# An FFT-convolution block on one core: transposing the filter ssm_k as 32-bit words instead of as bf16 elements

## The chip, the cores and the metric

One core of one Trainium2 chip. The core has five engines that run side by side and wait for one another by semaphores: TensorE (PE, with its weight loads shown apart as PEld), VectorE (DVE), ScalarE (ACT), GpSimd (POOL) and SyncE (SP), which issues most DMAs. SBUF is the working memory, 128 partitions wide; PSUM is where TensorE writes. The metric is the device time of one execution in microseconds (us), less is better. A time is the median of several executions.

## The reference

Shapes: S = 2048 time steps, D = 512 channels, all inputs bf16. In short:

```
kv = causal_conv4(k, shift_k) * v                  # 4 taps in time, per channel
y  = irfft(rfft(kv, 4096) * rfft(ssm_k, 4096))[:S] # long convolution in time, per channel
y  = y + kv * ssm_D
h  = q + layernorm(q) * y
out = h + relu(layernorm(h) @ w1) @ w2             # w1: 512 x 1376, w2: 1376 x 512
```

ssm_k is the long filter, 512 channels by 2048 steps. What this document is about is the start of the kernel, where ssm_k is read and brought into the layout that the Fourier transform needs.

## The kernel before

The program is written out in order by hand; each engine executes its own instructions in the order in which the code issues them, and waits where data or a place is missing. The stages that matter here:

- **Start (L95 to L252).** SP loads ssm_k into the tile `sk` (128 partitions x 4 channel groups x 2048 steps) in one DMA of 2 MB (L96). It then issues eight transposing DMAs, alternately for k (`kT`) and v (`vT`), a chunk of 512 steps each, and two small loads for ssm_D. While ssm_k loads, PE multiplies zeros (22 products, L110). POOL makes an identity (`ident`, L156 and L157), the tap matrices `wdiag` (L235), the first transform's tables `f1hi`, `f1lo`, `f2hi`, `f2lo`, and the negated sine table `c2n` (L247). DVE works out the angles for the sine tables (`cs_turns` L194, `_turns` L42, `cc_turns` L217, with `wrap` L186), and ACT evaluates sines (`table` L189, `_sin` L139).
- **Transposing ssm_k (L274 to L326).** `to_rows` is called for q = 0 to 7. Each call transposes eight 128x128 bf16 blocks on PE: block i holds the elements with step number 8q + i modulo 64, so the columns read from `sk` lie 64 elements apart. The eight results fill one PSUM bank, and one copy takes them into `kfl`, on DVE for even q and on ACT for odd q. For q = 3 and 4 the PSUM place is one of the two banks (`pk0`, `pk1`) that the taps use afterwards; the others take three places in turn, so q = 5, 6 and 7 wait for the copies of q = 0, 1 and 2.
- **Second half of the angles (L327).** `cc_turns(16)`, two instructions on DVE (L219, L187), stands behind these copies in DVE's order; one sine instruction (L328) stands behind them on ACT.
- **Taps and first transform stage (L340 to L358).** Eight rounds. In each, `taps` makes the 4-tap convolution on PE, in two PSUM banks, and DVE multiplies the result by v (L347), writing kv over `sk`. Then `stage1` transforms a part of `kfl` on PE, and ACT and DVE copy the result to `a1k`. A round's taps need the two banks that the round before used, so they wait for its L347.
- **Transposing kv (L380 to L392).** kv was written in pairs of neighbouring steps, so that 128 pairs lie side by side. A pair of bf16 elements is transposed as one 32-bit word (`kv32`, with a 32-bit identity `ident32` made at L338), four blocks of words per PSUM bank. The results go to `xfl`: on DVE as int32 with an OR by zero (L386), for q = 0, 2, 3, 5, 7, and on ACT as bf16 in two copies (L392), for q = 1, 4, 6.
- **The rest**: second transform stage of the filter (L398), first and second stages of kv, the products with the filter's transform, the inverse transform, and the two matrix products of the MLP with its layer norms, to the output DMAs.

The lines that the steps of the prediction speak of most are these:

```python
            nc.tensor.transpose(out=pst[:, i, :], in_=src[:, :, :, 8 * q + i], identity=ident[:])   # L278
        copy(eng, fl[:, :, :, 8 * q:8 * q + 8], pst[:].rearrange("p i (d g) -> p g d i", d=2))     # L279
...
        to_rows(skv, q, kfl, "DADADADA"[q])                                                        # L326
    cc_turns(16)                                                                                   # L327
```

Of the kernel before, what the change touches and what calls it, by code (L numbers as in the profile page):

```python
# [9 lines left out]
ALU = mybir.AluOpType  # L10
BF16 = mybir.dt.bfloat16
F32 = mybir.dt.float32
F32R = mybir.dt.float32r
I32 = mybir.dt.int32
PSUM = bass.MemoryType.PSUM
P = 128
# [40 lines left out]
def kernel(  # L57
# [13 lines left out]
    nc = tc.nc  # L71
    _, S, D = A_q.shape
# [15 lines left out]
    early = pl.push("early")  # L88
# [6 lines left out]
    sk = early.tile([P, DC, S], BF16, name="sk")  # L95
# [23 lines left out]
    for dp in range(2):  # L119
        src = bass.AP(tensor=A_ssm_D.tensor, offset=A_ssm_D.offset + 64 * dp, ap=[[0, 64], [P, DC], [1, 64]])  # L120
# [29 lines left out]
    for s in range(0, P, 64):  # L150
# [4 lines left out]
    ident = consts.tile([P, P], BF16, name="ident")  # L155
    nc.gpsimd.memset(ident[:], 0.0)  # L156
    nc.gpsimd.affine_select(out=ident[:], in_=ident[:], compare_op=ALU.not_equal, fill=1.0,  # L157
                            base=0, pattern=[[-1, P]], channel_multiplier=1)

    n1c = early.tile([P, 1], F32, name="n1c")  # L160
    n2c = early.tile([P, 1], F32, name="n2c")
# [55 lines left out]
    def cc_turns(a):  # L217
        part = tcs[:, a:a + 16, :]
        nc.vector.tensor_single_scalar(out=part, in_=tsn[:, a:a + 16, :], scalar=2048.0, op=ALU.add)  # L219
        wrap(part, 8192)  # L220
# [33 lines left out]
    def copy(eng, o, i):  # L254
        if eng == "A":
            nc.scalar.copy(out=o, in_=i)  # L256
        else:
            nc.vector.tensor_copy(out=o, in_=i)  # L258
# [4 lines left out]
    def place(shape, dtype, name):  # L263
        i = ring.pop(0)
        ring.append(i)
        return places[i].tile(shape, dtype, tag=f"ps{i}", name=name)
# [4 lines left out]
    def tap_bank(i, shape, dtype, name):  # L271
        return psum_t.tile(shape, dtype, tag=f"pk{i}", name=name)

    def to_rows(src, q, fl, eng):  # L274
        shape = [P, 8, P]
        pst = tap_bank(q % 5 - 3, shape, BF16, "pst") if q % 5 > 2 else place(shape, BF16, "pst")
        for i in range(8):
            nc.tensor.transpose(out=pst[:, i, :], in_=src[:, :, :, 8 * q + i], identity=ident[:])  # L278
        copy(eng, fl[:, :, :, 8 * q:8 * q + 8], pst[:].rearrange("p i (d g) -> p g d i", d=2))  # L279

    def stage1(fl, a_out, gb, engs, pairs=False):

# [38 lines left out]


    kfl = early.tile([P, 64, 2, 64], BF16, name="kfl")
    skv = sk[:].rearrange("p c (a b) -> p c a b", b=64)
    for q in range(8):
        to_rows(skv, q, kfl, "DADADADA"[q])  # L326
    cc_turns(16)  # L327
    _sin(dsc[:], t3[:], 64)  # L328
    dre = consts.tile([P, 2, 2, 64], F32R, name="dre")
# [4 lines left out]


    kvp2 = sk[:].rearrange("p c t -> p (c t)").rearrange("p (m c a e) -> p m c a e", m=32, c=DC, e=2)
    ident32 = early.tile([P, P], F32, name="ident32")
    nc.gpsimd.tensor_copy(out=ident32[:], in_=ident[:])  # L338

    def taps(c, h):  # L340
        pss = [tap_bank(i, [P, 512], F32, "pkv") for i in range(2)]
        for i in range(2):
            for j in range(KS):
                nc.tensor.matmul(out=pss[i][:], lhsT=wdiag[:, 2 * h + i, j, :],  # L344
                                 rhs=kT[c][:, 2 * h + i, 16 - j:CH + 16 - j], start=(j == 0), stop=(j == KS - 1))
        for i in range(2):
            nc.vector.tensor_tensor(out=kvp2[:, :, 2 * h + i, 8 * c:8 * c + 8, :].rearrange("p m a e -> p a m e"),  # L347
                                    in0=pss[i][:].rearrange("p (a m e) -> p a m e", a=8, e=2),
                                    in1=vT[c][:, 2 * h + i, :].rearrange("p (a m e) -> p a m e", a=8, e=2),
                                    op=ALU.mult)  # L350
# [24 lines left out]
    pl.pop("kvp")  # L375
    xfp = pl.push("xfp", side="right")
    xfl = xfp.tile([P, 64, 2, 64], BF16, name="xfl")
    kv32 = sk[:].rearrange("p c t -> p (c t)").bitcast(F32).rearrange("p (m x) -> p m x", m=32)
    xfl32 = xfl[:].rearrange("p g d n -> p (g d n)").bitcast(I32).rearrange("p (g d m) -> p g d m", g=64, d=2)
    for q in range(8):  # L380
        pst = place([P, 4, P], F32, "pst2")
        for i in range(4):
            nc.tensor.transpose(out=pst[:, i, :], in_=kv32[:, 4 * q + i, :], identity=ident32[:])  # L383
        ms = slice(4 * q, 4 * q + 4)
        if "DADDADAD"[q] == "D":
            nc.vector.tensor_single_scalar(out=xfl32[:, :, :, ms],  # L386
                                           in_=pst[:].bitcast(I32).rearrange("p m (d g) -> p g d m", d=2),
                                           scalar=0, op=ALU.bitwise_or)
        else:
            src = pst[:].rearrange("p m x -> p (m x)").bitcast(BF16).rearrange("p (m d g e) -> p d g m e", m=4, d=2, e=2)  # L390
            for d in range(2):
                nc.scalar.copy(out=xfl[:, :, d, 8 * q:8 * q + 8].rearrange("p g (m e) -> p g m e", e=2), in_=src[:, d])  # L392
    pl.pop("early")
    pl.pop("vp")
    slotB = pl.push("slotB")
# [437 lines left out]
```

## Time and profile before

| what | value |
|---|---|
| time, median of 3 runs | 208.6 us (208.33 to 209.07) |
| the profiled execution | 209.07 us, of which the span from the first to the last instruction is 206.9 us |
| granted TensorE clock | 0.998 of full speed |
| busy in the span | PE 195.4 us (94%), PEld 139.8 (68%), DVE 147.7 (71%), ACT 129.7 (63%), POOL 84.8 (41%) |
| ssm_k's transpositions on PE | start at 8.76 us, last 5.91 us |
| first taps after them | start at 14.51 us |
| second taps | start at 18.18 us |
| kv's transpositions on PE | start at 36.58 us |

How to read it: times are counted from the first instruction of the profiled execution. An engine that is busy for 94% of the span need not do useful work at its peak, since matmuls are pipelined and a waiting one can count as busy. The chain of waits names, going back from the last instruction, what each step waited for, so it tells which engine sets the end at each moment. A group line gives the line of code, the engine, the operation, the tiles out<-in, their shapes, how many there are, then the busy time and the mean duration of one in ns, and last the idle time of the engine ahead of them with what ended it.

### The profile page before, as it was taken

The page shows a single profiled execution, that of the slowest core. Times are in us where ns is not written, and L with a number is a line of the kernel's source. Part 1 is how long each engine was busy: PE and PEld are TensorE (multiplying, and loading weights), DVE is VectorE, ACT ScalarE, POOL GpSimd, SP SyncE. Part 2 cuts the span into 40 slices and gives each one's busy share as a digit, 9 for nine tenths or more (in the row PEclk, how much of TensorE's full clock was granted, in tenths as well). Part 3 has the DMA queues.
Part 4 walks back from the last instruction along what each step waited for, and adds up shares of the span by engine and source line. Part 5 has one row for each costly group of instructions (what it writes and reads, how often), then busy time and mean ns, then how long its engine had stood idle before and what let it go on. Part 6 is the DMA issues. An engine that isn't in the chain of part 4 may idle for free.

```text
span 206.9 us, 4925 instructions
## 1 busy us (share of the span) xinstructions
PE 195.4 (94%) x2017; PEld 139.8 (68%) x2017; DVE 147.7 (71%) x237; ACT 129.7 (63%) x196; POOL 84.8 (41%) x121
## 2 busy tenths in 40 slices
PE   7797999999996999999999999999999999999992
PEld 2494545899876799887999877645565556544451
DVE  7998777977686999988996599698297208561131
ACT  2676899845696688886896975753580494026300
POOL 4699991000001999997769655230202001102000
PEclk9999999999999999999999999999999999999999
DMA  5999960000000004835992557783753502040011
GB/s 179 339 220 188 197 126 5 3 3 0 3 3 2 5 0 122 203 154 148 197 287 49 108 101 56 165 156 97 138 100 77 119 13 54 27 103 22 0 54 51
DMA packets 48490, 20.03 MB, mean 97 GB/s; under 512 B 43380, under 2 KB 46932, under 8 KB 48468
## 3 DMA queue, kind: packets, MB, share of 16 engines
q1 hardware_dynamic: 47940, 19.71, 43.6%
q8 instruction: 16, 0.26, 0.5%
q10 hardware_dynamic: 528, 0.00, 0.1%
q14 instruction: 6, 0.05, 0.1%
HBM read 7.08 MB, written 2.10 MB: 44 GB/s over the span
## 4 chain that ended last, share of the span: by engine, by line
PE 82%; DVE 11%; ACT 3%; issue 1%; POOL 0%; POOLq 0%; ACTq 0%
PE ps1m L705 19%; PE ps2m L735 19%; PE psy L453 7%; PE psi L600 7%; PE pkv L344 6%; PE ps L299 4%; PE ps2k L317 4%; PE ps2k L319 4%; PE u L317 3%; PE u L319 3%; PE pz L678 3%; DVE kfl L258 2%; PE pst L383 2%; ACT a1x L256 1%; DVE w_ts L196 1%
## 5 line engine op out<-in xcount | busy, mean ns | idle before, releaser
L720 ACT ACTIVATE h1T<-ps1m 128x512 bf16<-128x512 f32 (+1 forms) x44 | 25.7, 597 | 35.8 <-PE ps1m L705 35.7
L705 PE MATMUL ps1m<-xT,w 128*128 128x512 bf16 (+2 forms) x192 | 43.7, 365 | 0.4 <-DVE xT L651 0.4
L735 PE MATMUL ps2m<-w,h1T 128*128 128x512 bf16 (+3 forms) x187 | 40.8, 368 | 0.0
L678 PE MATMUL pz<-bd,ax 128*128 128x128 f32 x96 | 35.7, 410 | 0.0
L443 POOL TENSOR_TENSOR t<-usb,kf 128x320 fp32r<-128x320 f32 x32 | 28.2, 937 | 2.3 <-ACT usb L439 1.9
L443 DVE TENSOR_TENSOR t<-u,kf 128x704 fp32r<-128x704 f32 x32 | 26.7, 887 | 3.4 <-ACT usb L439 3.4
L739 DVE SCALAR_TENSOR_TENSOR o<-ps2m,rstd,xh 128x512 bf16<-128x512 f32 (+1 forms) x17 | 12.0, 717 | 21.6 <-PE ps2m L735 10.1
L735 PEld LDWEIGHTS <-h1T 128*128 128x128 bf16 (+1 forms) x187 | 16.3, 98 | 16.0
L544 POOL TENSOR_SCALAR rstd<-mv 128x4 f32<-128x4 f32 x8 | 2.5, 317 | 56.5 <-DVE mv L542 56.5
L705 PEld LDWEIGHTS <-w 128*128 128x128 bf16 (+1 forms) x192 | 15.9, 100 | 12.1 <-DVE xT L651 0.5
L678 PEld LDWEIGHTS pz<-bd,ax 128*128 128x128 f32 x96 | 18.6, 193 | 7.6
L649 DVE TENSOR_TENSOR qT<-pz,qT 128x1024 bf16<-128x1024 f32 x8 | 9.8, 1219 | 15.1 <-PE pz L678 7.3
L538 DVE BATCH_NORM_STATS2 st<-xh 128x6 f32<-128x512 bf16 x32 | 19.8, 677 | 0.0
L256 ACT CAST kf<-psy 128x512 fp32r<-128x512 f32 x30 | 17.5, 644 | 1.9 <-PE psy L453 0.3
L528 ACT ACTIVATE bd<-ecw,nbias 32x512 fp32r<-32x512 int32 x24 | 17.3, 719 | 0.6
L344 PE MATMUL pkv<-kT,wdiag 128*128 128x512 bf16 x64 | 15.2, 380 | 1.2 <-DVE sk L347 1.2
L453 PE MATMUL psy<-t,ipos 128*128 128x512 f32 x48 | 16.0, 393 | 0.0
L256 ACT CAST a1k<-ps 128x1024 fp32r<-128x1024 f32 x12 | 12.8, 1112 | 3.1 <-PE ps L299 3.1
L256 ACT CAST ax<-psi 128x1024 fp32r<-128x1024 f32 x13 | 12.4, 1017 | 3.7 <-PE psi L600 3.7
L600 PE MATMUL psi<-dre,kf 128*128 128x256 f32 x60 | 14.6, 286 | 0.0
L600 PE MATMUL psi<-dim,kf 128*128 128x256 f32 x60 | 14.3, 280 | 0.0
L347 DVE TENSOR_TENSOR sk<-pkv,vT 128x512 bf16<-128x512 f32 x16 | 10.8, 689 | 4.3 <-PE pkv L344 4.3
(136 smaller groups left out, 419.4 us busy)
## 6 DMA issues: line engine op xcount, KB each, us to landing
sk<-in_A_ssm_k_dram SPq DMA_DIRECT2D x1, 2048.0 KB
xh<-in_A_q_dram SPq DMA_DIRECT2D x16, 128.0 KB
out_dram<-o SPq DMA_DIRECT2D x15, 128.0 KB
w<-in_B_w_dram SPq DMA_DIRECT2D x1, 1376.0 KB
w<-in_B_w_dram SPq DMA_DIRECT2D x1, 1280.0 KB
xh<-xT SPq DMA_TRANSPOSE x8
out_dram<-o SPq DMA_DIRECT2D x2, 64.0 KB
w<-in_B_w_dram SPq DMA_DIRECT2D x1, 96.0 KB
```

Of the source, the lines that this page charges most:

```text
L256: nc.scalar.copy(out=o, in_=i)
L317: nc.tensor.matmul(out=ps[:, kk, :], lhsT=at_k1(w_re, k1), rhs=a_in[:, k1, :], start=True, stop=False, skip_group_check=True)
L344: nc.tensor.matmul(out=pss[i][:], lhsT=wdiag[:, 2 * h + i, j, :], rhs=kT[c][:, 2 * h + i, 16 - j:CH + 16 - j], start=(j == 0), stop=(j == ...
L443: eng.tensor_tensor(out=t[:, :, j, :], in0=in0.unsqueeze(1).to_broadcast([P, 2, n, 2]), in1=kfr[:, :, j, ks], op=ALU.mult)
L453: nc.tensor.matmul(out=psy[:], lhsT=m_[:], rhs=t_.rearrange("p j k -> p (j k)"), start=first, stop=not first)
L528: nc.scalar.activation(out=bd[h][rows, :, :, rg, :], in_=ecw[q % 2][rows, :, 256 * h:256 * h + 256].rearrange("p b (j n) -> p b j n", n=32 ...
L538: nc.vector.bn_stats(out=st[:, i, :], in_=src[:, i, :])
L600: nc.tensor.matmul(out=banks[i // 2][:, i % 2, :], lhsT=kf[:, c, 4 * m:4 * m + 4, :].rearrange("p r k -> p (r k)"), rhs=d[:].rearrange("p ...
L678: nc.tensor.matmul(out=pz[:, il, :, a, :], lhsT=ax[:, 64 * rho + n2, :, :].rearrange("p d g -> p (d g)"), rhs=bd[h][:, rho, 4 * il + a, :, ...
L705: nc.tensor.matmul(out=ps1[fc][:fsz, 128 * ii.start:128 * ii.stop].rearrange("p (i t) -> p i t", t=P), lhsT=w1[:, c, fc * P:fc * P + fsz], ...
L720: nc.scalar.activation(out=h1T[:fsz, fc, :], in_=ps1[fc][:fsz, :], func=ACT.Relu)
L735: nc.tensor.matmul(out=ps2[:, 0:w], lhsT=h1T[:ksz, fc, i * P:(i + 1) * P], rhs=w2[:ksz, fc, ds], start=(fc == 0), stop=(fc == NFC - 1))
```

## The change

ssm_k is transposed in the way in which kv already was: two neighbouring steps (2m and 2m + 1) are one 32-bit word. `to_rows` makes four transpositions of 128x128 words for each q, with the identity `ident32`, and moves the words on DVE (int32, OR with zero) or ACT (bf16, two copies). The words of one block are read from `sk` at a distance of 32 words, since ssm_k lies as it was loaded. `to_rows` now serves both transpositions, with the same split over DVE and ACT ("DADDADAD"), so for ssm_k five moves are on DVE and three pairs on ACT, in place of four copies on each. The conversion that makes `ident32` moves up to the place where `ident` is made. Nothing else changes; the transposition of kv issues the same instructions.

```diff
     nc.gpsimd.affine_select(out=ident[:], in_=ident[:], compare_op=ALU.not_equal, fill=1.0,
                             base=0, pattern=[[-1, P]], channel_multiplier=1)
+    ident32 = early.tile([P, P], F32, name="ident32")
+    nc.gpsimd.tensor_copy(out=ident32[:], in_=ident[:])
...
-    def to_rows(src, q, fl, eng):
-        shape = [P, 8, P]
-        pst = tap_bank(q % 5 - 3, shape, BF16, "pst") if q % 5 > 2 else place(shape, BF16, "pst")
-        for i in range(8):
-            nc.tensor.transpose(out=pst[:, i, :], in_=src[:, :, :, 8 * q + i], identity=ident[:])
-        copy(eng, fl[:, :, :, 8 * q:8 * q + 8], pst[:].rearrange("p i (d g) -> p g d i", d=2))
+    def to_rows(word, q, fl, eng):
+        shape = [P, 4, P]
+        pst = tap_bank(q % 5 - 3, shape, F32, "pst") if word is sk_word and q % 5 > 2 else place(shape, F32, "pst")
+        for i in range(4):
+            nc.tensor.transpose(out=pst[:, i, :], in_=word(4 * q + i), identity=ident32[:])
+        if eng == "D":
+            fl32 = fl[:].rearrange("p g d n -> p (g d n)").bitcast(I32).rearrange("p (g d m) -> p g d m", g=64, d=2)
+            nc.vector.tensor_single_scalar(out=fl32[:, :, :, 4 * q:4 * q + 4],
+                                           in_=pst[:].bitcast(I32).rearrange("p m (d g) -> p g d m", d=2),
+                                           scalar=0, op=ALU.bitwise_or)
+        else:
+            src = pst[:].rearrange("p m x -> p (m x)").bitcast(BF16).rearrange("p (m d g e) -> p d g m e", m=4, d=2, e=2)
+            for d in range(2):
+                nc.scalar.copy(out=fl[:, :, d, 8 * q:8 * q + 8].rearrange("p g (m e) -> p g m e", e=2), in_=src[:, d])
...
-    skv = sk[:].rearrange("p c (a b) -> p c a b", b=64)
+    sk32 = sk[:].rearrange("p c t -> p (c t)").bitcast(F32).rearrange("p (x m) -> p x m", m=32)
+    kv32 = sk[:].rearrange("p c t -> p (c t)").bitcast(F32).rearrange("p (m x) -> p m x", m=32)
+
+    def sk_word(m):
+        return sk32[:, :, m]
+
     for q in range(8):
-        to_rows(skv, q, kfl, "DADADADA"[q])
+        to_rows(sk_word, q, kfl, "DADDADAD"[q])
...
-    ident32 = early.tile([P, P], F32, name="ident32")
-    nc.gpsimd.tensor_copy(out=ident32[:], in_=ident[:])
...
     for q in range(8):
-        pst = place([P, 4, P], F32, "pst2")
...
+        to_rows(lambda m: kv32[:, m, :], q, xfl, "DADDADAD"[q])
```

More of the change, by code (lines that the diff above doesn't have):

```diff
@@ L377 @@
     xfl = xfp.tile([P, 64, 2, 64], BF16, name="xfl")
-    kv32 = sk[:].rearrange("p c t -> p (c t)").bitcast(F32).rearrange("p (m x) -> p m x", m=32)
-    xfl32 = xfl[:].rearrange("p g d n -> p (g d n)").bitcast(I32).rearrange("p (g d m) -> p g d m", g=64, d=2)
     for q in range(8):
-        pst = place([P, 4, P], F32, "pst2")
[L382 to L392, printed above, removed]
+        to_rows(lambda m: kv32[:, m, :], q, xfl, "DADDADAD"[q])
     pl.pop("early")
```

## The prediction

> **What bounds the kernel now.** I read the share of each engine first (PE 94%, DVE 71%, ACT 63%, POOL 41%), then the chain of waits over the first 37 us, because every line of the change that executes differently lies there. The chain, in order of time (start, length, what):
>
> ```profile
> 10.38 0.69 DVE w_tc L187
> 11.07 4.52 DVE kfl L258 x4
> 15.59 1.22 DVE w_tc L219
> 16.90 0.55 issue
> 17.45 0.69 DVE sk L347
> 18.18 1.89 PE pkv L344 x8
> ```
>
> The reader is to see that until 18.18 us the end is set by DVE: table arithmetic to 11.07, its four copies of transposed ssm_k, more table arithmetic (L219, then L187 from 16.84 to 17.53), and the first product L347. That product frees the PSUM bank that TensorE's second group of taps needs, so PE starts again at 18.18. From there on the chain is PE, nearly without a gap, and a shift of 18.18 passes to the end. The groups of instructions of this stage, and of the later stage that already transposes words, give the prices (busy us, mean ns | idle before):
>
> ```profile
> L278 PEld LDWEIGHTS <-sk 128*128 128x128 bf16 x64 | 5.8, 201 | 1.6 <-DMA sk<-in_A_ssm_k_dram 1.6
> L344 PEld LDWEIGHTS <-wdiag 128*128 128x128 bf16 x64 | 5.8, 98 | 7.2 <-issue 1.1
> ...
> L258 DVE COPY kfl<-pst 128x1024 bf16<-128x1024 bf16 x4 | 4.6, 1212 | 0.0
> L256 ACT COPY kfl<-pst 128x1024 bf16<-128x1024 bf16 x4 | 4.1, 1018 | 2.9 <-PE pst L278 2.9
> ...
> L383 PEld LDWEIGHTS pst<-ident,sk 128*128 128x128 f32 x32 | 3.4, 141 | 0.6 <-issue 0.3
> L386 DVE TENSOR_SCALAR xfl<-pst 128x512 int32<-128x512 int32 x5 | 3.4, 687 | 0.3
> ...
> L392 ACT COPY xfl<-pst 128x512 bf16<-128x512 bf16 x6 | 3.1, 596 | 0.5 <-DVE a1k L258 0.3 <-PE pst L383 0.2
> ```
>
> And two stretches of the timeline of PE (start, length, what, how many):
>
> ```profile
> 8.76 5.91 PE L278 MATMUL pst<-ident,sk 128*128 128x128 bf16 x64 [1.06 <-DMA sk<-in_A_ssm_k_dram]
> ```
> ```profile
> 36.58 1.06 PE L383 MATMUL pst<-ident,sk 128*128 128x128 f32 x8 [0.26 <-DVE sk L347]
> ```
>
> Each bf16 transposition takes (5.91-0.25)/63 = 0.09 us, each 32-bit one (1.06-0.27)/7 = 0.11 us. But their loads differ: L278 reads sk with 64 elements (128 bytes) between columns, and its load shows 201 ns; L344 reads adjacent columns of the same size and shows 98. The 32-bit loads of L383 read adjacent words (141 ns).
>
> **The change, part by part.**
>
> *Copies.* Removed: 4 DVE copies, 4.52 us on the chain, and 4 of ACT. Added: 5 DVE moves like L386 (four of them took 37.56 to 40.37, so 0.70 each), 3.50 us, and 3 pairs on ACT like L392 at 1.07 a pair. If the data is always there, DVE ends its copies at 11.07 + 3.50 = 14.57 instead of 15.59: **1.02 us earlier**. ACT is not the bound: three pairs are 3.2 us against 4.1.
>
> *Transpositions.* 64 bf16 ones go, 32 of words come, reading sk with the same 128 bytes from column to column. **This operation is not in the trace.** Call its pace p. The last batch (q = 7) goes to DVE, so DVE's copies end at the later of 14.57 and 8.76 + 32p + 0.25 (drain of the last matmul, 0.27 long, and the semaphore) + 0.70. The second is the later from p = 0.152; at p = 0.184 it is 15.60, where nothing is won or lost.
> From below, p = 0.11, the word load with adjacent columns: sk's bf16 loads touched 128 places in 0.09 us, so 0.11 is possible. From above, the load duration of a strided tile against an adjacent one, 201/98 = 2.05, taken on the 32-bit load's 141 ns, with nothing overlapped: 0.29. In between lie 0.201 (the strided load's own duration) and 0.11 x 2.05 = 0.226. I take **0.215**, between these two: the strided load of sk is the only row that reads this tile with this step, and the word loads have no spare time (their pace of 0.11 is not set by the 128-column matmul, since the bf16 ones go at 0.09 with the same matmul). Then DVE ends at 8.76 + 6.88 + 0.25 + 0.70 = 16.59, **1.00 us later** than 15.59.
>
> [...]
>
> *Behind the copies on DVE* stand L219, L187 and L347 in both kernels, 15.59 to 18.14, so 18.18 moves with them. L219 took 0.81 us at 9.53 and 1.29 at 15.51, both 128x1024, beside different POOL work. If it meets the short POOL copies (which end at 15.11) rather than the long c2n one (from 15.20), up to 0.48 comes off. That can only happen when DVE is earlier, at 14.57; when it is later, POOL is in c2n as now.
>
> *PSUM.* Places are as before: q = 5, 6, 7 take those of q = 0, 1, 2. At p = 0.215 none of them waits: q5's place is free at 11.77, and PE reaches q5 at 13.06. At 0.11, PE waits for DVE's q0 (11.77) and q2 (12.47), sends q7 at about 13.2, ready 13.5, before DVE comes for it at 13.87.
>
> *TensorE behind the transpositions.* Taps(0,0), 1.84 us, follow them, then the first stage-1 group (0.65), both done by about 18.2 at p = 0.215, while L347 ends at 19.14. So the DVE chain still sets the restart, and the 1.00 is counted once.
>
> *ident32* moves on POOL from 23.71 to 2.87, 0.28 us. POOL there had nothing until wsh lands (2.45 us idle before 5.63), so this costs nothing; without that cover it would push wdiag by 0.28, which PE needs only after 13. The first transposition now waits for it, done near 3.2, and for sk at 8.76: the DMA is the later. Taking it from 23.71 brings the last c2n piece forward by 0.28; stage 2 wants that only after 40.
>
> *DMAs.* None is added or moved, SP's order is the same. By the landing events kT0 lands at 10.92, vT0 at 13.41, kT3 at 27.38, vT3 at 30.83. The first product of chunk 3 starts at 32.63, so an earlier schedule has 1.8 us before DMA bites, more than any gain here.
>
> *Instruction supply.* PE had one stop of 0.36 us for no named cause at 30.82, inside stage 1. PE's program has 96 fewer instructions (128 become 32), so such a stop may vanish or fall elsewhere: plus or minus 0.36. I take nothing. The stage that transposes kv (L383) issues the same instructions as before.
>
> *Sum.* -1.02 for the copies, +2.02 because the last data reaches DVE at 15.89 rather than 13.87: **+1.0 us** on the profiled run's 209.07 (span 206.9, 2.2 around it). That run stands 0.47 above the median of the three, 208.6. I forecast 209.6 for the median.
>
> **The rivals.**
> 1. *Words at the pace of adjacent words* (faster). If the step of 128 bytes costs the word load nothing (p up to 0.152), DVE ends its copies at 14.57, and PE restarts 1.0 earlier, up to 1.5 with the shorter L219: 207.1 to 207.6, say 207.5. For it: 128 places in 0.09 us. Against it: that load's 201 ns against 98, and a pace that was uneven there, though steady at 0.11 in L383. **35%**.
> 2. *Between* (no change). p from 0.164 to 0.204 moves the end by under 0.63 us, 0.3%, about what a measurement of this kernel can tell: 208.0 to 209.2, say 208.6. **12%**.
> 3. *The forecast*, p from 0.204 to 0.24: 209.2 to 210.4 by the same sum, without the instruction stop. **40%**.
> 4. *Loads that no longer overlap*, p near 0.29: 8.76 + 9.28 + 0.95 = 18.99, 3.4 later, 212.0. For it: two of sk's bf16 loads are always under way (201 long, 90 apart), and the 32-bit ones overlap less (141 long, 109 to 113 apart). Against it: they overlap somewhat. **13%**.
>
> **How the numbers follow.** Faster by over 0.3%: rival 1, 0.35. Within: rival 2, 0.12. Slower: 0.40 + 0.13 = 0.53. The likeliest single case is the forecast, 209.6, with its own range of 209.2 to 210.4. The range for 8 in 10 must take in rival 1, since gains and losses are close in chance: 207.1. It leaves out most of rival 4 and reaches 211.0 (p of 0.26).
>
> **What would show it.** In the changed kernel's group list, the new word load of sk: near 141 ns and a stretch under 5 us for 32 transpositions is rival 1; a stretch of 6.5 to 7.5 us is the forecast; over 9 is rival 4. In the chain, five kfl moves on DVE of 0.70 without gaps (rival 1) or with waits for pst among them (forecast). The second taps group starts at 17.2 or earlier (rival 1), 19.2 (forecast). The stretch from there to the end must keep its length, about 188.7 us. I am wrong if TensorE reads these words as fast as adjacent ones, or if that stretch changes by more than the 0.36 us stop.

## The result, and the profile after

The changed kernel takes 206.81 us (206.56 to 207.15, 4 runs), the kernel before 208.66 us in the same comparison: a ratio of 0.9911, with a 95% interval of 0.9888 to 0.9935. It is about 0.9% faster, where the forecast was 209.6 us, slower, with a range from 207.1 to 211.0. The profiled execution took 206.56 us with a span of 204.4 us, against 209.07 and 206.9.

The gain is where the prediction looked for it, only with the other sign: the second group of taps starts at 16.33 us instead of 18.18. The timeline of PE after the change (start, length, what, how many, idle time before with what ended it):

```profile
8.87 2.48 PE L280 MATMUL pst<-ident,sk 128*128 128x128 f32 x20 [0.32 <-DMA sk<-in_A_ssm_k_dram]
12.01 1.61 PE L280 MATMUL pst<-ident,sk 128*128 128x128 f32 x12 [0.66 <-DVE kfl L283]
...
16.33 1.89 PE L356 MATMUL pkv<-kT,wdiag 128*128 128x512 bf16 x8 [0.37 <-POOL f_lo L246]
```

Twenty word transpositions go through at once; then PE waits, for a place and not for its loads. The first twenty last 2.48 us, of which 0.28 is the length of the last one: **0.116 us each**. The other twelve go once DVE has emptied a place. The name behind the last line is a trap: a wait is put down to the semaphore that came last, and here DVE's first L359 (the old L347) ends at 16.27, 0.06 before the restart, as it ended at 18.13, 0.05 before the restart, in the kernel before, where POOL's copies had been done since 15.11. The taps read nothing that L246 writes. The timeline of DVE in the same stretch, before and then after:

```profile
10.99 4.61 DVE L258 COPY kfl<-pst 128x1024 bf16<-128x1024 bf16 x4
15.51 1.29 DVE L219 TENSOR_SCALAR w_tc<-w_ts 128x1024 int32<-128x1024 int32 x1
16.84 0.69 DVE L187 TENSOR_SCALAR w_tc<-w_tc 128x1024 int32<-128x1024 int32 x1
17.45 1.28 DVE L347 TENSOR_TENSOR sk<-pkv,vT 128x512 bf16<-128x512 f32 x2
```

```profile
10.66 0.69 DVE L189 TENSOR_SCALAR w_tc<-w_tc 128x1024 int32<-128x1024 int32 x1
11.27 3.08 DVE L283 TENSOR_SCALAR kfl<-pst 128x512 int32<-128x512 int32 x5
14.26 0.68 DVE L221 TENSOR_SCALAR w_tc<-w_ts 128x1024 int32<-128x1024 int32 x1
14.98 0.69 DVE L189 TENSOR_SCALAR w_tc<-w_tc 128x1024 int32<-128x1024 int32 x1
15.59 1.28 DVE L359 TENSOR_TENSOR sk<-pkv,vT 128x512 bf16<-128x512 f32 x2
```

Five moves back to back, no wait for `pst` among them, then the angles and the first product. Against the lines of before: DVE comes to the copies 0.28 later (11.27 against 10.99), needs 2.99 instead of 4.52 for them (-1.53), and 1.33 instead of 1.94 for the two angle instructions (-0.61). Together that is -1.86, which is the whole of 18.18 to 16.33 within rounding. From the restart to the end the span loses another 0.6: the round of the first stage in which PE had stopped (0.36 at 30.82 before) is 0.33 shorter (1.15 before, 0.82 after, from its first product to the next taps), and the stretch of the products with the filter's transform, in which ACT had stopped, is 0.3 shorter (see e11). The groups of instructions from 8.5 to 14 us (busy us, mean ns | idle before):

```profile
L280 PEld LDWEIGHTS pst<-ident,sk 128*128 128x128 f32 x32 | 3.7, 194 | 1.6 <-DVE kfl L283 0.8 <-issue 0.8
L289 ACT COPY kfl<-pst 128x512 bf16<-128x512 bf16 x6 | 3.2, 589 | 2.0 <-PE pst L280 2.0
L283 DVE TENSOR_SCALAR kfl<-pst 128x512 int32<-128x512 int32 x5 | 3.1, 681 | 0.0
```

The strided word load shows 194 ns, where the adjacent word load of kv shows 141. Its duration is longer, as expected, and its pace hardly is (0.116 against 0.113 in the prediction's row of kv): that is the riddle that the experiments had to solve.

### The profile page after: what moved, and what is told of

It reads as the page before. It is cut to its first block, busy times and chain, and to the rows that moved or that the text cites. A ratio compares the mean times of both kernels' runs of the same rounds, so it can differ in the third digit from the quotient of the medians.

```text
span 204.4 us, 4868 instructions
## 1 busy us (share of the span) xinstructions
PE 194.5 (95%) x1985; PEld 138.0 (68%) x1985; DVE 146.0 (71%) x238; ACT 128.7 (63%) x198; POOL 86.6 (42%) x121
## 4 chain that ended last, share of the span: by engine, by line
PE 83%; DVE 5%; ACT 5%; POOL 4%; issue 1%; POOLq 0%; ACTq 0%
PE ps1m L704 19%; PE ps2m L734 19%; PE psy L452 7%; PE psi L599 7%; PE pkv L356 6%; PE ps L309 4%; PE ps2k L327 4%; PE ps2k L329 4%; PE u L327 3%; PE u L329 3%; PE pz L677 3%; PE pst L280 2%; ACT c2s L193 1%; ACT a1x L258 1%; POOL wdiag L237 1%; DVE a1x L260 1%
## 5 line engine op out<-in xcount | busy, mean ns | idle before, releaser
L359 DVE TENSOR_TENSOR sk<-pkv,vT 128x512 bf16<-128x512 f32 x16 | 10.8, 689 | 4.4 <-PE pkv L356 4.2
```

## The experiments

Two theories stood at the start. **A**: the gain is DVE's chain alone, five short moves in place of four long copies. **B**: the start has two limits one behind the other, the pace of the bf16 transpositions and the copies, and words move both. A landmark helps in all of them: the restart (start of the second taps group). One thing disturbs it. The small DMA of `wsh` (the tap weights, issued by ACT) lands early in some executions and late in others, just behind ssm_k: POOL's `wdiag`, which waits for it, starts at 5.6 to 5.8 us or at 9.2 to 9.4. When it lands early, two small angle instructions on DVE run beside `wdiag` and take 0.90 and 1.09 us (before, at 5.83 and 6.64) instead of 0.18 and 0.25; when it lands late, DVE is spared that and reaches its copies 1.0 to 1.5 us earlier. It was early in the first profiles of both kernels, in e5 and in e9's kernel before, late in the other profiles of e1 to e11, and the last group of runs was made for it. A profile shows one execution of several, so a median can hold both kinds.

### e1: word loads with adjacent columns

```diff
-        return sk32[:, :, m]
+        return kv32[:, m, :]
```

> The changed kernel with the words of ssm_k read side by side instead of 128 bytes apart (so the filter's steps are permuted). Theory A (the step of 128 bytes costs a word load no pace; the gain came from DVE's shorter chain): 206.8, within 0.3% of the changed kernel, and 20 words still take 2.3 to 2.5 us on PE. Theory S (the step does cost something that is on the path): faster than the changed kernel by 0.5 us or more, 206.3 or less. In the profile: if the 201 ns of sk's bf16 loads came from the step, the word loads here show 141 ns; if it came from the DMAs and copies that run beside them, they stay near 190.

Measured: 207.15 us, 0.9906 (0.9871 to 0.9941). The 32 transpositions show this load:

```profile
L280 PEld LDWEIGHTS pst<-ident,sk 128*128 128x128 f32 x32 | 3.5, 141 | 1.6 <-issue 1.6
```

The pace without a step is 0.110 us (32 in 3.69 us), with it 0.115 (32 in 3.83 us in the changed kernel of e9, where `wsh` is late as here). The step costs the word load 53 ns of duration and 5 ns of pace. So a load's duration is not its price: these loads overlap (141 ns long and 110 apart, or 194 long and 115 apart), and how far can't be read off one row.

### e2: bf16 loads with adjacent columns (in the kernel before)

```diff
-    skv = sk[:].rearrange("p c (a b) -> p c a b", b=64)
+    skv = sk[:].rearrange("p c t -> p (c t)").rearrange("p (b c a) -> p c a b", c=DC, a=32)
```

> The kernel before with the bf16 columns of ssm_k read side by side (filter steps permuted). Theory A: the same time as before, 208.7 within 0.3%, because DVE sets the restart; PE's 64 transpositions shrink from 5.9 us or stay waiting for places. Rival P (PE's stretch of transpositions set the end): faster by 1 us or more, below 207.7. In the profile: a load near 98 ns and a shorter stretch says that the step costs the bf16 loads pace; near 200 ns says that it does not come from the step.

Measured: 207.70 us, 0.9947 (0.9919 to 0.9975). Its groups from 8.5 to 15 us:

```profile
L258 DVE COPY kfl<-pst 128x1024 bf16<-128x1024 bf16 x4 | 4.6, 1218 | 0.3 <-PE pst L278 0.3
...
L278 PEld LDWEIGHTS <-sk 128*128 128x128 bf16 x64 | 3.6, 98 | 0.7 <-DMA sk<-in_A_ssm_k_dram 0.7
```

Here the same step of 128 bytes does cost pace: 64 transpositions last 3.75 us, 0.056 each, against 0.090 with the step (64 in 5.91). DVE's four slow copies run unchanged and still 0.9 us of time goes. The restart lies where e9's changed kernel, with words and short moves, has it (e2 and then e9):

```profile
16.33 1.89 PE L344 MATMUL pkv<-kT,wdiag 128*128 128x512 bf16 x7 [1.25 <-DVE sk L347]
```
```profile
16.32 1.89 PE L356 MATMUL pkv<-kT,wdiag 128*128 128x512 bf16 x8 [1.10 <-POOL f_hi L246]
```

(Where a line shows x7 for the eight products of a group, one record is missing from the trace.) That speaks against A: PE's pace was a limit too, at least when DVE comes to the copies early, as in this run (9.64), and there it was the one that counted.

### e3, e10: words on PE, copies like the old ones

```diff
+        if fl is kfl:
+            copy(eng, fl[:, :, :, 8 * q:8 * q + 8].rearrange("p g d (m e) -> p g d m e", e=2),
+                 pst[:].rearrange("p m x -> p (m x)").bitcast(BF16).rearrange("p (m d g e) -> p g d m e", m=4, d=2, e=2))
...
-        to_rows(sk_word, q, kfl, "DADDADAD"[q])
+        to_rows(sk_word, q, kfl, "DADADADA"[q])
```

e10 is the same with `p g d e m` on both sides, so that the innermost step skips every other element.

> The changed kernel's word transpositions of ssm_k, but moved by four bf16 copies of 1024 elements on DVE and four on ACT, as before. Theory A (the gain is DVE's): all of it is lost and the early identity costs 0.3 more: 208.7 to 209.2. Rival P (the gain is PE's: 32 transpositions for 64, fewer instructions): 206.8 to 207.3.

> The changed kernel's word transpositions, moved by four copies on DVE and four on ACT whose innermost steps skip every other element, so that DVE is to take 1.1 to 1.2 us a copy, as before, where the earlier experiment's copies of neighbouring pairs turned out to take 0.69. Theory B: with PE fast and DVE slow, DVE's four copies last 4.5 us back to back, and about half the gain is lost: 207.4 to 208.2. If the moves cost nothing that matters (theory P): 206.6 to 207.3.

Measured: e3 207.39 us, 0.9944 (0.9906 to 0.9982); e10 207.74, 0.9963 (0.9943 to 0.9983). The first did not isolate what it was made for, since its copies were not the old ones any more. The DVE copies of the two, e3 and then e10:

```profile
L260 DVE COPY kfl<-pst 128x1024 bf16<-128x1024 bf16 x4 | 2.8, 692 | 0.8 <-PE pst L280 0.8
```
```profile
L260 DVE COPY kfl<-pst 128x1024 bf16<-128x1024 bf16 x4 | 4.6, 1218 | 0.2 <-PE pst L280 0.2
```

A bf16 copy that takes neighbouring pairs needs 692 ns for 1024 elements, as long as an int32 move of the same bank (681); the order of the elements, not the type, makes the 1212 ns of before (1218 in e10, bf16 as in e3). e10 is the clean test, and in it the slow copies cost the restart little: 16.49, against 16.32 in the changed kernel of e9. Its copies end at 14.43, the moves of the changed kernel at 13.60, and still only 0.17 is left at the restart, because there L221 meets POOL's `wdiag` sum and takes 1.42 us, where e10's takes 0.77. So with `wsh` late, most of the words' gain comes through PE: the kernel before restarts at 17.49 there (e11). (e10 takes 207.74 against 207.57, and it has the 0.3 us stop of e11, as the kernel before does.)

### e4: bf16 transpositions, the new moves

```diff
...
+            for i in range(8):
+                nc.tensor.transpose(out=pst[:, i, :], in_=skv[:, :, :, 8 * q + i], identity=ident[:])
+            pst = pst[:].rearrange("p i x -> p (i x)").bitcast(F32).rearrange("p (m x) -> p m x", m=4)
...
```

> The reverse: the 64 bf16 transpositions of before, moved by the changed kernel's five int32 moves on DVE and three pairs of ACT copies (the moves read the bank as if it held words, so the filter's elements land in a wrong order). Theory A: most of the gain stays, less what DVE waits for the last batch, which PE now sends at about 14.7 instead of 13.6: 207.3 to 207.8. Rival P: 208.5 or more.

Measured: 208.48 us, 0.9978 (0.9948 to 1.0008): no difference that can be told. DVE's timeline shows why:

```profile
9.90 0.69 DVE L289 TENSOR_SCALAR kfl<-pst 128x512 int32<-128x512 int32 x1 [0.26 <-PE pst L281]
11.40 0.69 DVE L289 TENSOR_SCALAR kfl<-pst 128x512 int32<-128x512 int32 x1 [0.81 <-PE pst L281]
12.26 0.69 DVE L289 TENSOR_SCALAR kfl<-pst 128x512 int32<-128x512 int32 x1 [0.16 <-PE pst L281]
13.96 0.69 DVE L289 TENSOR_SCALAR kfl<-pst 128x512 int32<-128x512 int32 x1 [1.01 <-PE pst L281]
15.41 0.69 DVE L289 TENSOR_SCALAR kfl<-pst 128x512 int32<-128x512 int32 x1 [0.76 <-PE pst L281]
```

The short moves wait for PE in every line, and the last bank comes at 15.41; the restart is this line, later than the 17.49 that the old copies reach with `wsh` late:

```profile
18.09 1.89 PE L363 MATMUL pkv<-kT,wdiag 128*128 128x512 bf16 x7 [0.37 <-DVE sk L366]
```

Two things burden e4 besides: with the new split DVE takes the last bank (q = 7), which ACT took before, and the 64 transpositions last 6.45 us instead of 5.91, for no cause that the trace names. So faster copies alone brought nothing, and **theory A falls** where `wsh` is late. e2 and e10 show that PE's pace is the limit there; that DVE's copies are the limit when `wsh` is early is read from the lines of before (four copies back to back, no wait for `pst`), and no run changed them alone in that state.

### e5, e6, e7, e8: the angles later, ident32 on ACT

`cc_turns(16)` was moved behind the second round's `negated` in the kernel before (e5) and in the changed one (e6); e7 makes `ident32` on ACT; e8 does both in the changed kernel.

```diff
-    cc_turns(16)
...
+            cc_turns(16)
```
```diff
-    nc.gpsimd.tensor_copy(out=ident32[:], in_=ident[:])
+    nc.scalar.copy(out=ident32[:], in_=ident[:])
```

> The kernel before with its second half of the angles (L219 and L187, 1.9 us on DVE) moved behind the second round of taps. Theory A (DVE's chain sets the restart of PE at 18.18): L347 starts 1.9 us earlier, PE restarts as soon as its first stage-1 group ends, near 17.0: 207.4 to 207.7. Rival (what is moved is only paid later on DVE, or the restart hangs on something else): 208.5 or more.

> The changed kernel with the same move. Theory A: PE restarts at 15.9, where its first stage-1 group ends, instead of 16.33: 206.3 to 206.5. Rival: no change from 206.8, or slower if DVE's sums come to fall in front of something else.

> The changed kernel with the 32-bit identity converted on ACT, which idles until 5.5, instead of on POOL, where the conversion took 1.56 us beside DVE's table sum and DVE's next instruction 1.16 instead of 0.89. Theory A: DVE gets to its moves 0.28 earlier, at 11.07: 206.4 to 206.6. Rival (the 0.28 is scatter of DVE, or ACT's table load is pushed back and takes it): 206.8 or more.

> Both moves in the changed kernel. Theory A: DVE's first move ends 0.28 earlier, so PE's sixth to eighth batches, taps and first stage-1 group do too, and PE restarts at 15.6: 206.0 to 206.3. Rival: no better than the better of the two.

Measured: e5 210.24 us, 1.0076 (1.0055 to 1.0096); e6 207.67, 0.9950 (0.9928 to 0.9972); e7 207.66, 0.9951 (0.9929 to 0.9972); e8 207.84, 0.9955 (0.9934 to 0.9977). The restart did come earlier (17.03 in e5, against 18.18; 15.29 in e6, 16.11 in e7 and 15.22 in e8, against 16.32), and nothing of it can be told in the time. Among the taps every L347 is waited for, so in e5, e6 and e8 the two angle instructions hold PE up there as they did at the start (in e5 they run at 21.32 and 22.22): from the restart to kv's transpositions e5 needs 20.3 us instead of 18.4, e6 and e8 20.5 instead of 18.9. The place tried was no free slot of DVE; others were not tried. In these three profiles the filter's second stage also lasts 15.34 us instead of 14.79, but not for want of sines: its products follow one another every 118 ns instead of 113, with no wait, and so they do in a profile of e13 whose angles are in the old place. What slows them is not known. e7 can't be told from the changed kernel run again (207.57).

### e9, e11: both kernels again, and two more instructions on ACT

e9 runs both kernels unchanged. e11 adds to the kernel before two tiny copies on ACT whose results nobody reads:

```diff
+    for _ in range(2):
+        nc.scalar.copy(out=f1f[:, 0:1], in_=nbias[:])
```

> The changed kernel as it is, beside the next three on one chip: 206.6 to 207.3. If wsh (the small load that POOL's tap matrices wait for) lands near 9.2 here, as it did in seven of the eight experiments, and not near 5.5 as in the first two traces, DVE should reach its first move near 9.8 and PE should restart its second taps near 16.6, no earlier than in the first trace (16.33), since then POOL holds up the table sums behind the moves.

> The kernel before as it is, for its trace: 208.4 to 208.8. If wsh lands near 9.2, DVE starts its copies near 9.8 and theory B (two limits in a row: PE sends bf16 batches until 14.5, and DVE's copies last 1.13 each) has DVE waiting for PE between its copies, and PE restarting at 17.5 to 18.2, so that the late landing buys the old kernel little. Theory A (DVE's copies alone): the copies run back to back and the restart comes at 16.8.

> The kernel before with two 128x1 copies more on ACT, behind the filter's copies, and nothing else: the changed kernel has two ACT instructions more than before, and in every trace with them an 8 KB instruction fetch lies near 55 to 57 us instead of at the start of the product stage, where ACT then stops for 0.3. Theory I (instruction fetch): that fetch moves to 55 to 57, the stretch from the first product to the 65th shrinks from 14.0 to 13.7, and the time falls by 0.3 us from before, to 208.3. Rival: no change or slower by the copies' 0.1.

Measured: changed 207.57 us, 0.9952 (0.9924 to 0.9980); before 208.93, 1.0009 (0.9973 to 1.0046); e11 208.27, 0.9975 (0.9950 to 0.9999). The gain of the change is 1.3 us here, not 1.9. In the changed kernel's profile `wsh` is late, and though the restart is again at 16.32, the stretch from there to the second filter stage lasts 22.6 us instead of 21.8: PE and DVE now wait for `kT` and `vT`. Its chain has a piece that the first profile has not:

```profile
23.33 6.64 DMA kT<-in_A_k_dram
29.98 0.05 issue
30.02 1.90 PE pkv L356 x8
```

This is not only an earlier PE meeting the same DMA: that last `kT` was issued 2.1 us later than before (23.33 against 21.22) and landed 2.6 later (29.98 against 27.38). In e2, a bf16 kernel, it was issued at 24.20, so the words are not needed for it; why it differs between executions was not settled.

e11 shows the stop of ACT. The products' stretch (from the first to the 65th product) lasts 14.0 us in the kernel before (e9's too), in e2, e3, e5 and e10, whose ACT executes as many instructions; it lasts 13.7 in the changed kernel and in e11, e1, e4, e6 and e9's changed one, with two more, and in e7 and e8, with four more. The first copies of that stage on ACT, before and then e11:

```profile
66.98 0.85 ACT L439 COPY usb<-u 128x160 f32<-128x160 f32 x3 [1.49 <-PE u L319]
```
```profile
65.76 0.70 ACT L441 COPY usb<-u 128x160 f32<-128x160 f32 x2 [1.17 <-PE u L319]
```

In the kernel before, ACT stands 1.49 us idle before three copies in a row, which had piled up; with two more instructions it starts after 1.17, with two. That is 0.3 us that the change gets by accident: two copies that nobody reads bring it too. (e11's whole time can't be read as the price of the stop, since `wsh` was late in its profile.) The bf16 kernels of the next group, with one instruction fewer on ACT than before, are at 13.7 as well, so more instructions are not needed. The expectation named an 8 KB instruction fetch as the cause. It did move with e11, from 65.6 us, the start of this stretch, to 56.0; but those bf16 kernels have it at 64.7 and 65.7, again at the start of the stretch, and no stop. What causes the stop was not settled.

### e13: wsh's place fixed, four kernels

`wsh` is issued by SP instead of ACT, directly behind ssm_k (meant to land late in every execution) or directly ahead of it (early); the four profiles have it so:

```diff
-    nc.scalar.dma_start(out=wsh[:], in_=A_shift_k.rearrange("(r p) j -> p r j", p=P))
+    nc.sync.dma_start(out=wsh[:], in_=A_shift_k.rearrange("(r p) j -> p r j", p=P))
```

> The kernel before with the small load wsh issued on SP behind ssm_k's, so that it always lands near 9.2 and POOL's tap matrices start only then. Theory B (two limits in a row): DVE reaches its first copy near 9.9, waits for PE's bf16 batches between its copies and ends them near 15.5; PE restarts near 17.5. Time 208.0 to 208.8. Theory A (DVE's copies alone): copies back to back, ended at 14.4, restart 16.8, time 207.3.

> The changed kernel with the same move: first DVE move near 9.8, last ends near 13.6, PE restarts at 16.3 to 16.7; then up to 0.9 us goes to waits for kT and vT, which land no earlier than before. 207.0 to 207.7, so 0.8 to 1.3 under its partner.

> The kernel before with wsh issued on SP ahead of ssm_k's load, which then starts about 0.5 later. wsh lands near 5.5, POOL's tap matrices hold up DVE's table sums, DVE starts its copies at 11.1 and runs them back to back to 15.6 to 15.7, PE restarts at 18.2 to 18.4. 208.6 to 209.4.

> The changed kernel with wsh ahead: DVE's moves from 11.3 back to back to 14.4, PE restarts near 16.4, as in its first trace; 206.8 to 207.6, so 1.6 to 2.2 under its partner, against 0.8 to 1.3 with wsh behind.

Measured, each against the unchanged kernel before (208.67):

| | bf16 as before | words | the change |
|---|---|---|---|
| `wsh` ahead | 209.09, 1.0032 (1.0011 to 1.0053), restart 18.60 | 207.33, 0.9942 (0.9926 to 0.9958), restart 16.28 | -1.76 us |
| `wsh` behind | 207.98, 0.9966 (0.9949 to 0.9984), restart 17.45 | 207.11, 0.9934 (0.9916 to 0.9951), restart 16.33 | -0.87 us |

The four restarts, bf16 and words with `wsh` ahead, then bf16 and words with it behind:

```profile
18.60 1.89 PE L344 MATMUL pkv<-kT,wdiag 128*128 128x512 bf16 x7 [1.01 <-DVE sk L347]
16.28 1.89 PE L356 MATMUL pkv<-kT,wdiag 128*128 128x512 bf16 x7 [0.37 <-POOL f_lo L246]
```
```profile
17.45 1.89 PE L344 MATMUL pkv<-kT,wdiag 128*128 128x512 bf16 x7 [0.16 <-POOL f_lo L244]
16.33 1.89 PE L356 MATMUL pkv<-kT,wdiag 128*128 128x512 bf16 x7 [1.27 <-POOL f_hi L246]
```

The products' stretch lasts 13.7 us in all four, so the 0.3 of ACT's stop is not in these differences. With `wsh` ahead, DVE is late and its copies lie all but back to back (10.80 to 15.79, with one wait of 0.18), DVE binds, and the words bring the restart 2.32 forward. Part of that is given back before the second stage, 22.6 us from the restart against 21.8. With `wsh` behind, DVE comes at 9.99 and PE binds, as the kernel before's DVE timeline shows, and the words bring the restart 1.12 forward:

```profile
9.99 1.23 DVE L258 COPY kfl<-pst 128x1024 bf16<-128x1024 bf16 x1 [0.60 <-PE pst L278]
11.41 1.23 DVE L258 COPY kfl<-pst 128x1024 bf16<-128x1024 bf16 x1 [0.20 <-PE pst L278]
12.85 1.22 DVE L258 COPY kfl<-pst 128x1024 bf16<-128x1024 bf16 x1 [0.21 <-PE pst L278]
14.25 1.23 DVE L258 COPY kfl<-pst 128x1024 bf16<-128x1024 bf16 x1 [0.18 <-PE pst L278]
```

Every copy waits for its bank; 1.4 us lie between them, two banks of eight bf16 transpositions. Both limits end within about a microsecond of each other: here PE's sets 17.45, and words on PE with slow copies restart at 16.49 (e10). With `wsh` late, releasing the copies alone gave nothing (e4) and releasing PE alone nearly all of the restart (e2, e10). The change moves both, so it gains in either case, 0.9 to 1.8 us. (The profile of the words with `wsh` behind, at 207.56 the slowest of its six executions, is the one with the second stage at 118 ns a product.) Changed with `wsh` behind is the fastest version of these (207.11), but it isn't told apart from the changed kernel as it is (206.81 and 207.57 in two comparisons).

## Why the prediction was wrong, step by step

- **The pace p, the step that failed.** The prediction took 0.215 us for a word load with a step of 128 bytes. It is 0.116 (0.110 without the step, e1). The 0.215 came from the load's duration, "201 ns against 98", carried to the words as if a duration were a pace. But bf16 loads of 201 ns go at 0.090 and word loads of 194 ns at 0.116, so 2.2 and 1.7 of them are under way at a time. The premise that carried it was that "the word loads have no spare time". They had: 141 ns at 0.110 is only 1.3 under way, and with the step the overlap rose instead of the pace. The reason given for the premise, that the bf16 transpositions "go at 0.09 with the same matmul", falls with e2: without the step they go at 0.056, so 0.09 was itself the price of the step and said nothing about the matmul. What does set the words' 0.11, about twice 0.056, no run shows. The row that the prediction put at the lower end, kv's words at 0.11, was the right one. That the bf16 loads do lose pace by the step (e2) made the wrong reading look right.
- **The sum around it held.** Its formula gives, for p up to 0.152, "1.0 earlier, up to 1.5 with the shorter L219" at the restart; measured 1.85. Rival 1 (207.1 to 207.6) is what happened: its mark, a stretch under 5 us and five moves without gaps, is in the profile. The 206.81 lies a little below it, and below the range of 8 in 10. (One slip without consequence: by the prediction's own sum, p of 0.204 moves the end by 0.65, not by under 0.63.)
- **Terms off in size.** The move: 0.70 priced, 0.60 measured back to back (2.99 for five), since the row's four moves held waits between them: -0.5. L219: up to 0.48 off was allowed, 0.61 came off with L187, under the condition given (L219's instruction lay beside POOL's short copies and took 0.68 us, where it had taken 1.29 beside `c2n`). ident32 "costs nothing": no, +0.28. POOL's conversion took 1.56 us instead of 0.28, beside two of DVE's table instructions, of which the second, L189, took 1.15 instead of 0.89, and DVE came that much later to all that follows. With the conversion on ACT (e7) the same L189 takes 0.89 again, and DVE is 0.24 earlier at the instruction ahead of its moves (8.70 against 8.94 in e9):

```profile
2.94 1.56 POOL L160 CAST ident<-ident 128x128 f32<-128x128 bf16 x1
```
```profile
4.38 1.15 DVE L189 TENSOR_SCALAR w_ts<-w_ts 128x1408 int32<-128x1408 int32 x1
```

- **PSUM.** Right at this pace: PE waits for DVE's first place (0.66 before 12.01) and sends the last bank in time, so the wait costs nothing.
- **DMAs.** "1.8 us before DMA bites" did not hold in every execution: in e9's profile the chain runs through `kT` at 29.98, and the earlier restart is partly given back. The margin took the landings of one profile as fixed; that `kT` landed at 27.38 there.
- **Instruction supply.** The plus or minus 0.36 was named for PE, where some 0.3 went; another 0.3 went on ACT, which was not named at all. The stretch from the restart to the end, which "must keep its length, about 188.7 us", became 188.1, more than the 0.36 allowed. Without these two, the first comparison would lie inside rival 1 (about 207.4, an estimate from these differences); that it lies below is luck as far as the change is concerned.
- **The missing limit.** The prediction saw PE's bf16 pace only as a row to learn from. When `wsh` lands late it is the bound (e13), and the gain is 0.9 instead of 1.8. Nothing in the one profile of before showed that.

Left open: why `wsh` lands early in some executions and late in others; what causes the stops of PE and ACT and the slower second stage of four profiles; what the moves alone, or PE's pace alone, bring when `wsh` is early; and the adjacent bf16 order together with the new moves, which was not tried.

## What to carry to other kernels

Price an instruction whose neighbours overlap, as these loads do, by the distance between starts in a stretch without waits, not by its duration: here 98 to 201 ns of duration went with 0.056 to 0.090 us of pace (bf16), and 141 to 194 ns with 0.110 to 0.115 (words). When two engines feed each other, ask of each limit when it would end if the other were free: here they ended about a microsecond apart, and an edit that moves only the one that isn't last brings nothing (e4), where one that moves the other brings nearly all (e2). And run both kernels more than once before reading 0.3 us: here a stop that came and went with two instructions was worth 0.3 us (e11), and the gain of the change was 0.87 or 1.76 us by where a small DMA landed (e13).

## What the runs showed of the hardware beyond that

- TensorE's loads of 128x128: a step of 128 bytes between columns took bf16 from 0.056 (e2) to 0.090 us of pace (before; 98 to 201 ns shown), 32-bit words from 0.110 (e1) to 0.115 (e9; 141 to 194 ns).
- DVE's copy of 1024 bf16 elements a partition out of PSUM: 692 ns with neighbouring pairs innermost (e3), 1212 to 1218 without (before, e2, e10).
- An instruction of 128x1024 on DVE (L221) took 0.68 us beside POOL's short copies (the changed kernel's first profile), and 1.42 (e9) and 1.58 (e13, words with `wsh` behind) beside POOL's `wdiag` sum, with the same operands. In e3 it took 0.78 beside that sum, and the L189 behind it took 1.41 instead of 0.69.
- A DMA of a few words for each partition, issued beside a 2 MB load, let its reader start at 5.6 us in one execution of the changed kernel (its first profile) and at 9.2 in another (e9), with nothing changed in the program.
